# One weight conversion moved into the seam between two attention batches, and half of a scaling given to GpSimd

## The chip, the cores and the metric

The kernel runs on one core of one Trainium2 chip. The metric is the device time of one execution in microseconds; before the change it is 471.23 us (median of 3 runs, 470.49 to 472.06).

## The reference

Three blocks follow each other.

1. Attention over q, k, v of shape (2 batches, 8 heads, 576 positions, 64 wide): scores `q k^T / 8` plus a linear bias per head, masked to a causal window of 128 positions; softmax over the keys; times v.
2. A gated layer on the 1152 tokens: `a = x w1`, `b = x w2`, then `(a * b) w3 w_out`. The weights of this block arrive in float64.
3. A mixture of 8 experts: each token goes to the expert with the largest gate logit, `relu(x w1_e) w2_e`, scaled by the gate's probability.

```python
scores = np.where(mask, scale * q @ k.T + bias, -1e9)
attn = np.exp(scores - scores.max(-1)); attn /= attn.sum(-1) + 1e-9
x = attn @ v                                  # block 1
x = ((x @ w1) * (x @ w2)) @ w3 @ w_out        # block 2
out[i] = gate_w[i] * (relu(x[i] @ e1[e]) @ e2[e])   # block 3, e = argmax of the logits
```

## The kernel before

**Precision.** Matrix products of blocks 2 and 3 use a high part and a low part of each float32 operand: three products (high times high, high times low, low times high) accumulate in one PSUM bank.

**A weight conversion.** A float64 weight chunk (128 x 512) is loaded by the sync queue and turned into its two parts by `convert` (line 126). It has three pieces. `begin` (line 135) is one ScalarE instruction. `bits` (lines 138 to 140) is three VectorE instructions: a shift, an and-or, a shift-or. `parts` is a ScalarE cast that writes the high part (line 71, tile `wh`), a GpSimd subtraction that writes the low part (line 72, tile `wl`), and the issue of the next load (`stage_next`, line 101). The weights w1 and w2 make 16 chunks, four for each quarter `c` of the hidden width: two for w1 and two for w2. Four are converted during batch 0, the other twelve during batch 1. For those, the list `CONVS` (line 24) says how many each of batch 1's twelve steps takes.

**Attention steps.** Steps are numbered k = 0 to 23; batch 1 is k = 12 to 23. A step handles two heads and the row blocks (0, 1), (2, 3) or (4). Its work is spread over neighbouring steps. TensorE makes the scores one step ahead (`att_qk(k + 1)`), VectorE takes the maximum (`att_max`, line 248), ScalarE the exponential with its row sum (`att_exp`, line 259). One step later `att_norm(k)` forms the reciprocals (lines 277, 278) and, in batch 1 only, scales the probabilities: one VectorE instruction for each block and head (line 287), so four in a step with two blocks and two in a step with one. `att_tr(k)` (line 301) then transposes the probabilities on TensorE, ScalarE copies them out of PSUM (line 303) and `att_pv(k)` (line 321) multiplies by v.

**Filling work.** In batch 1 TensorE also computes block 2's first products for batch 0 (`ab_half`, lines 376 to 378), 32 units of 12 products each. Units alternate between w1 (m = 0, the result is copied by ScalarE, line 383) and w2 (m = 1, the result is multiplied into `g` by VectorE, line 388). Unit number u needs the chunks of quarter u // 8. So the first unit of quarter 1 (unit 8) falls in step 15 and unit 9, which needs quarter 1's third and fourth chunk, is the first unit of step 16; unit 16 opens step 19.

**Order.** [...] From step 14 on TensorE's order in a step is: one unit, the transposes of k - 1, the scores of k + 1, one unit (two where k % 3 is 2), the products with v of k - 1. VectorE's is: maxima of block one, scaling of k - 1, maxima of block two, then `bits`, with the g products between. GpSimd has only the subtractions of `parts` in this stretch. Step 13 is alike; the seam, k = 12, ends batch 0 (its last scaling, transposes, products with v and split of the attention output) while it begins batch 1.

Names used below: "the subtraction" is GpSimd's line 72, "the scaling" is line 287, tr(k) is the group of transposes of step k on line 301, pv(k) the products with v on line 321.

Of the kernel before, what the change touches and what calls it, by code (L numbers as in the profile page):

```python
# [20 lines left out]
BIGS = 31  # L21
STAGES = 4
WARM = (4, 4, 4, 2, 2, 2, 2, 2, 2, 2, 2)
CONVS = (0, 1, 1, 2, 1, 1, 2, 1, 1, 1, 1, 0)
OOB = 1 << 20


# [1 line left out]
def block_kernel(ctx: ExitStack, tc: tile.TileContext, qT, kT, v, w1, w2, w3T, wo, wg, e1, e2, out):  # L29
    nc = tc.nc  # L30
# [36 lines left out]
    def ps(tag, name):  # L67
        return psum.tile([P, 512], F32, tag=tag, name=name, bufs=2)
# [8 lines left out]
    def keep_clock(n, name):  # L77

        w = ps("t", name)
        for _ in range(n):  # L80
            nc.tensor.matmul(w, hot[:, :P], hot, start=True, stop=True)  # L81
# [78 lines left out]
    def load_qk(b, hp):  # L160
        h0 = 2 * hp
        t = slot(f"qk_{b}_{hp}", (2, S), F32)
        for i, src in enumerate((qT, kT)):
            nc.sync.dma_start(out=t[:, i, :], in_=src[b, h0 : h0 + 2].rearrange("h d s -> (h d) s"))
        vt = apool.tile([P, 6, P], F32, tag="v", name=f"v_{b}_{hp}", bufs=3)
        cs = slice(h0 * D, (h0 + 2) * D)
        nc.sync.dma_start(out=vt[:, 0:4, :], in_=v[b, 0 : 4 * P, cs].rearrange("(c p) d -> p c d", p=P))
        nc.sync.dma_start(out=vt[:TK, 4:6, :], in_=v[b, S - 2 * TK : S, cs].rearrange("(c p) d -> p c d", p=TK))
        qk[b, hp] = t, vt
# [38 lines left out]
    def conv_w(c, m, kp):  # L208
        if kp == 0:
            wsb[m, c] = slot(f"wh{m}_{c}", (KD, WC)), slot(f"wl{m}_{c}", (KD, WC))  # L210
        return convert(("w", c, m, kp), *(w[:, 2 * kp : 2 * kp + 2, :].rearrange("p k f -> p (k f)") for w in wsb[m, c]), pool_hi=(c == 0))
# [12 lines left out]
    def att_qk(k):  # L224
        b, hp, g = groups[k]
        t = qk[b, hp][0]
        tag = "acc" if k <= NGB and k % 2 else "s"
        sps = [ps(tag, f"s{j}_{k}").rearrange("p (i w) -> p i w", i=2) for j in range(2)]
        for gj, i in enumerate(g):
            q0, M, k0, W, _, _ = blocks[i]  # L230
            for j in range(2):
                js = slice(j * D, (j + 1) * D)
                nc.tensor.matmul(sps[j][:M, gj, :W], t[js, 0, q0 : q0 + M], t[js, 1, k0 : k0 + W], start=True, stop=True)  # L233
        live["s", k] = sps

    def att_max(k, gj):
        b, hp, g = groups[k]
        if gj == 0:
            live["p", k] = [], apool.tile([P, 12], F32, tag="sm", name=f"stat_{k}", bufs=8)
        pp, st = live["p", k]  # L240
        i = g[gj]
        q0, M, k0, W, _, _ = blocks[i]
        off = P - (q0 - k0)
        p = apool.tile([P, 2, 2 * P], F32, tag="p", name=f"p_{k}_{i}", bufs=6)
        pp.append(p)
        for j in range(2):
            c = 2 * gj + j
            nc.vector.tensor_tensor_reduce(out=p[:M, j, :W], in0=live["s", k][j][:M, gj, :W],  # L248
                                           in1=relb[:M, 2 * hp + j, off : off + W], scale=-1.0 / isq, scalar=3.0e38,
                                           op0=ALU.add, op1=ALU.min, accum_out=st[:M, c : c + 1])  # L250

    def att_exp(k, gj):
        b, hp, g = groups[k]
        pp, st = live["p", k]
        p = pp[gj]
        _, M, _, W, _, _ = blocks[g[gj]]
        for j in range(2):
            c = 2 * gj + j
            nc.scalar.activation(out=p[:M, j, :W], in_=p[:M, j, :W], func=AF.Exp, scale=-1.0,  # L259
                                 bias=st[:M, c : c + 1], accum_out=st[:M, 4 + c : 5 + c])  # L260
# [11 lines left out]
    def att_norm(k):  # L272
        b, hp, g = groups[k]
        pp, st = live["p", k]
        n = 2 * len(g)
        M = blocks[g[0]][1]
        nc.vector.tensor_scalar_add(st[:M, 8 : 8 + n], st[:M, 4 : 4 + n], 1e-9)
        nc.vector.reciprocal(st[:M, 8 : 8 + n], st[:M, 8 : 8 + n])
        if b == 0:
            for gj, i in enumerate(g):  # L280
                factor[hp, i] = st[:, 8 + 2 * gj : 10 + 2 * gj]
            return
        for gj, i in enumerate(g):
            p, W = pp[gj], blocks[i][3]
            for j in range(2):
                c = 8 + 2 * gj + j
                nc.vector.tensor_scalar_mul(p[:M, j, :W], p[:M, j, :W], st[:M, c : c + 1])

    def att_tr(k):
        b, hp, g = groups[k]  # L290
        pp, _ = live.pop(("p", k))
        pts = []
        for gj, i in enumerate(g):
            _, M, _, W, C, _ = blocks[i]
            nh = W // C
            tp = ps("t", f"t_{k}_{i}")
            pt = apool.tile([P, 2, 2, P], F32, tag="pt", name=f"pt_{k}_{i}", bufs=4)
            tpv = tp.rearrange("p (j n q) -> p j n q", j=2, n=2)
            for j in range(2):
                for n in range(nh):  # L300
                    nc.tensor.transpose(tpv[:C, j, n, :M], pp[gj][:M, j, n * C : (n + 1) * C], ident[:M, :M])  # L301
            copy = nc.vector.tensor_copy if b == 0 and i in (1, 3) else nc.scalar.copy
            copy(out=pt[:C, :, :nh, :M], in_=tpv[:C, :, :nh, :M])
            pts.append(pt)
        live["pt", k] = pts
# [52 lines left out]
    def att_fin():  # L358
        if fins:
            fins.pop(0)()  # L360
# [5 lines left out]
    def ab_half(b, f, ch, m, tag="acc", part=None):  # L366
        c, fs = f // (WC // P), slice(f * P % WC, f * P % WC + P)
        n = slice(ch * NCH, (ch + 1) * NCH)
        if part != 1:
            live["ab", m] = ps(tag, f"ab{m}_{b}_{f}_{ch}")  # L370
        a = live["ab", m]
        for kt in (range(KD), range(KD - 1), range(KD - 1, KD))[0 if part is None else 1 + part]:
            hi, lo = (w[:, kt, :] for w in wsb[m, c])
            xh, xl = xs_[b, kt]
            first, last = kt == 0, kt == KD - 1
            nc.tensor.matmul(a[:, :NCH], hi[:, fs], xh[:, n], start=first, stop=False)  # L376
            nc.tensor.matmul(a[:, :NCH], hi[:, fs], xl[:, n], start=False, stop=False)  # L377
            nc.tensor.matmul(a[:, :NCH], lo[:, fs], xh[:, n], start=False, stop=last)  # L378
        if part == 0:
            return  # L380
        if m == 0:
            asb = cv.tile([P, NCH], F32, tag="asb", name=f"asb_{b}_{f}_{ch}")
            nc.scalar.copy(out=asb, in_=a[:, :NCH])  # L383
            live["asb"] = asb
        else:
            if f % 2 == 0 and ch == 0:
                gt[b, f // 2] = slot(f"g_{b}_{f // 2}", (2, S), F32)
            nc.vector.tensor_tensor(out=gt[b, f // 2][:, f % 2, n], in0=a[:, :NCH], in1=live["asb"], op=ALU.mult)  # L388
# [259 lines left out]
    def conv_next():  # L648
        return conv_w(*wq.pop(0)) if wq else None
# [10 lines left out]
    for k in range(NGB):  # L660
# [3 lines left out]
        cvt = conv_next() if k in (2, 5, 8, 10) else None  # L664
# [36 lines left out]
    for k in range(NGB, 2 * NGB):  # L701
        b, hp, g = groups[k]
        if g[0] == 2 and hp + 2 < NPAIR:
            load_qk(1, hp + 2)
        if k == NGB:

            att_fin()
            att_norm(k - 1)
            att_tr(k - 1)
            att_pv(k - 2)  # L710
            att_pv(k - 1)

            for u in ab0[:2]:
                ab_half(*u, part=0)
            begun = ab0[:2]
            att_max(k, 0)
            att_exp(k, 0)
            att_fin()
            att_max(k, 1)
            att_exp(k, 1)  # L720
            att_fin()
            att_qk(k + 1)
            keep_clock(3, "warm_b")
            fill(ab0, 1)
        elif k == NGB + 1:
            att_soft(k, lambda: (att_norm(k - 1), fill(ab0, 1)))
            att_fin()
        else:
            att_soft(k, lambda: att_norm(k - 1))
            att_fin()  # L730
        cvts = [c for c in (conv_next() for _ in range(CONVS[k - NGB])) if c]
        for c in cvts:
            c[0]()
        if k > NGB:
            fill(ab0, 1)
            att_tr(k - 1)
        if NGB < k < 2 * NGB - 1:
            att_qk(k + 1)
        for c in cvts:
            c[1]()  # L740
        if k > NGB:
            fill(ab0, 2 if k % 3 == 2 else 1)
        for c in cvts:
            c[2]()
        if k > NGB:
            att_pv(k - 1)
# [199 lines left out]
```

## Time and profile before

| | |
|---|---|
| median of 3 runs | 471.23 us |
| the profiled execution's own time | 470.63 us |
| its span, first to last instruction | 468.9 us |
| TensorE busy | 452.7 us |
| VectorE busy | 319.9 us |
| ScalarE busy | 261.4 us |
| GpSimd busy | 147.1 us |
| mean granted TensorE clock | 0.988 |

Busy time counts an engine's instructions; an engine can be busy and yet late, where its instruction waits for a port or runs at the lower clock. The profiled execution is one of several; its own time lies 0.60 us under the median of the runs, within their spread.

### The profile page before, as it was taken

The page shows a single profiled execution, that of the slowest core. Times are in us where ns is not written, and L with a number is a line of the kernel's source. Part 1 is how long each engine was busy: PE and PEld are TensorE (multiplying, and loading weights), DVE is VectorE, ACT ScalarE, POOL GpSimd, SP SyncE. Part 2 cuts the span into 40 slices and gives each one's busy share as a digit, 9 for nine tenths or more (in the row PEclk, how much of TensorE's full clock was granted, in tenths as well). Part 3 has the DMA queues.
Part 4 walks back from the last instruction along what each step waited for, and adds up shares of the span by engine and source line. Part 5 has one row for each costly group of instructions (what it writes and reads, how often), then busy time and mean ns, then how long its engine had stood idle before and what let it go on. Part 6 is the DMA issues. An engine that isn't in the chain of part 4 may idle for free.

```text
span 468.9 us, 9276 instructions
## 1 busy us (share of the span) xinstructions
PE 452.7 (97%) x3339; PEld 405.3 (86%) x3346; DVE 319.9 (68%) x860; ACT 261.4 (56%) x653; POOL 147.1 (31%) x154
## 2 busy tenths in 40 slices
PE   8999999989999999999999999999999999999993
PEld 4667887868899999999999999588889898898982
DVE  6786768787542454888756777257878787888840
ACT  5786756565432345443545554056777677676740
POOL 2135113212111133344311211123465453544531
PEclk9999998989999999999999999999999999999998
DMA  8855325322159444675422444338796977868001
GB/s 267 248 187 177 101 85 178 113 71 87 47 176 237 132 133 136 204 298 154 146 75 69 136 136 136 114 130 275 259 288 196 310 230 248 278 205 291 27 1 54
DMA packets 30769, 77.77 MB, mean 166 GB/s; under 512 B 3582, under 2 KB 9214, under 8 KB 30720
## 3 DMA queue, kind: packets, MB, share of 16 engines
q1 hardware_dynamic: 28976, 72.41, 50.0%
q0 software_dynamic: 1744, 4.73, 2.7%
q8 instruction: 28, 0.46, 0.4%
q14 instruction: 21, 0.17, 0.1%
HBM read 65.30 MB, written 12.61 MB: 166 GB/s over the span
## 4 chain that ended last, share of the span: by engine, by line
PE 78%; DVE 10%; issue 5%; ACT 3%; POOL 2%; DVEq 0%; POOLq 0%; ACTq 0%
PE h L580 10%; PE ab L376 7%; PE ab L378 7%; PE ab L377 6%; PE h L581 4%; PE x L474 4%; PE x L475 4%; PE x L476 4%; PE warm L81 4%; DVE t_w L140 3%; PE t L301 3%; PE s L233 3%; PE oa L321 3%; PE y L609 3%; PE y L612 3%
## 5 line engine op out<-in xcount | busy, mean ns | idle before, releaser
L72 DVE TENSOR_TENSOR le<-st_e,he 128x1024 fp32r<-128x1024 f32 x64 | 78.4, 1226 | 28.1 <-ACT he L71 23.8
L376 PE MATMUL ab<-x,wh 128*128 128x288 f32 x256 | 80.3, 314 | 0.8 <-ACT wh L71 0.7
L595 POOL CAST hs<-hs 128x64 fp32r<-128x64 f32 x64 | 55.3, 871 | 76.5 <-ACT hs L591 75.3
L580 PE MATMUL h<-xs,he 128*128 128x384 f32 x256 | 76.8, 358 | 2.2 <-DVE xs L72 2.2
L378 PE MATMUL ab<-x,wl 128*128 128x288 f32 x256 | 76.4, 299 | 1.2 <-POOL wl L72 1.1
L377 PE MATMUL ab<-x,wh 128*128 128x288 f32 x256 | 76.0, 297 | 0.0
L71 ACT CAST he<-st_e 128x1024 fp32r<-128x1024 f32 x64 | 67.3, 1051 | 0.0
L581 PE MATMUL h<-xs,le 128*128 128x192 f32 x256 | 64.2, 251 | 0.0
L376 PEld LDWEIGHTS ab<-x,wh 128*128 128x128 f32 x256 | 48.6, 190 | 6.4 <-issue 2.3
L580 PEld LDWEIGHTS h<-xs,he 128*128 128x128 f32 x256 | 48.0, 188 | 5.2 <-DVE xs L72 2.6
L581 PEld LDWEIGHTS h<-xs,le 128*128 128x128 f32 x256 | 48.8, 191 | 1.9
L378 PEld LDWEIGHTS ab<-x,wl 128*128 128x128 f32 x256 | 48.6, 190 | 2.0 <-POOL wl L72 2.0
L377 PEld LDWEIGHTS ab<-x,wh 128*128 128x128 f32 x256 | 48.7, 190 | 0.0
L388 DVE TENSOR_TENSOR g<-ab,asb 128x288 f32<-128x288 f32 x32 | 14.6, 456 | 48.0 <-PE ab L378 45.7
L259 ACT ACTIVATE p<-p,stat 128x256 f32<-128x256 f32 (+2 forms) x80 | 37.3, 470 | 13.0 <-DVE stat L248 13.0
L474 PE MATMUL x<-wph,gh 128*128 128x260 f32 x144 | 41.4, 287 | 0.0
L476 PE MATMUL x<-wph,gl 128*128 128x260 f32 x144 | 40.6, 282 | 0.0
L475 PE MATMUL x<-wpl,gh 128*128 128x260 f32 x144 | 40.6, 282 | 0.0
L588 ACT COPY cr<-h 128x192 f32<-128x192 f32 x64 | 20.5, 320 | 35.3 <-PE h L581 33.2
L383 ACT COPY asb<-ab 128x288 f32<-128x288 f32 x32 | 12.7, 397 | 47.8 <-PE ab L378 47.8
L440 PE MATMUL wp<-woh,w3h 128*128 128x260 f32 x128 | 36.3, 284 | 0.5 <-DVE wpl L72 0.5
L442 PE MATMUL wp<-woh,w3l 128*128 128x260 f32 x128 | 36.2, 283 | 0.0
(139 smaller groups left out, 1074.5 us busy)
## 6 DMA issues: line engine op xcount, KB each, us to landing
st_e<-e SPq DMA_DIRECT2D x64, 512.0 KB, 4.3
st_w<-w SPq DMA_DIRECT2D x16, 512.0 KB, 4.5
st_w<-w3T SPq DMA_DIRECT2D x16, 512.0 KB, 4.0
disp<-zrow SPq DMA_DIRECT2D x1, 4626.0 KB, 22.1
st_wo<-wo SPq DMA_DIRECT2D x8, 512.0 KB, 3.6
qk<-qT SPq DMA_DIRECT2D x8, 288.0 KB, 5.2
qk<-kT SPq DMA_DIRECT2D x8, 288.0 KB, 5.6
y<-zrow SPq DMA_DIRECT2D x1, 2304.0 KB, 10.9
```

The source lines that it names most:

```text
L71: nc.scalar.copy(out=hi, in_=t)
L72: eng.tensor_tensor(out=lo, in0=t, in1=hi.bitcast(F32), op=ALU.subtract)
L259: nc.scalar.activation(out=p[:M, j, :W], in_=p[:M, j, :W], func=AF.Exp, scale=-1.0, bias=st[:M, c : c + 1], accum_out=st[:M, 4 + c : 5 + c])
L376: nc.tensor.matmul(a[:, :NCH], hi[:, fs], xh[:, n], start=first, stop=False)
L377: nc.tensor.matmul(a[:, :NCH], hi[:, fs], xl[:, n], start=False, stop=False)
L378: nc.tensor.matmul(a[:, :NCH], lo[:, fs], xh[:, n], start=False, stop=last)
L474: nc.tensor.matmul(pa[:, :HG], gh[:, kt, :], th, start=(kt == 0), stop=False)
L475: nc.tensor.matmul(pa[:, :HG], gh[:, kt, :], tl, start=False, stop=False)
L476: nc.tensor.matmul(pa[:, :HG], gl[:, kt, :], th, start=False, stop=(kt == KF - 1))
L580: nc.tensor.matmul(hp_[:, : 2 * N0], hi[:, kt, fs], xs, start=(kt == 0), stop=False)
L581: nc.tensor.matmul(hp_[:, N0 : 2 * N0], lo[:, kt, fs], xs[:, :N0], start=False, stop=(kt == KD - 1))
L595: nc.gpsimd.tensor_copy(h[:, 2 * N0 :], h[:, P:N0])
```

## The change

`CONVS` changes, so that batch 1 converts two chunks in a step once (step 14) and no longer twice (steps 15 and 18). The first of the twelve is taken in the seam, with its three pieces at three places between the seam's softmax parts. And in the scaling of batch 1 the second head of each block (j = 1) is given to GpSimd, the first stays on VectorE.

```diff
-CONVS = (0, 1, 1, 2, 1, 1, 2, 1, 1, 1, 1, 0)
+CONVS = (0, 1, 2, 1, 1, 1, 1, 1, 1, 1, 1, 0)
...
                 c = 8 + 2 * gj + j
-                nc.vector.tensor_scalar_mul(p[:M, j, :W], p[:M, j, :W], st[:M, c : c + 1])
+                (nc.gpsimd if j else nc.vector).tensor_scalar_mul(p[:M, j, :W], p[:M, j, :W], st[:M, c : c + 1])
...
             begun = ab0[:2]
+            cvt = conv_next()
+            cvt[0]()
             att_max(k, 0)
             att_exp(k, 0)
+            cvt[1]()
             att_fin()
             att_max(k, 1)
             att_exp(k, 1)
             att_fin()
+            cvt[2]()
             att_qk(k + 1)
```

Chunks converted by the end of each step of batch 1, k = 12 to 22: before 0, 1, 2, 4, 5, 6, 8, 9, 10, 11, 12; after 1, 2, 4, 5, 6, 7, 8, 9, 10, 11, 12.

## Rows read from the trace of the kernel before

**Rows 1.** The page: TensorE's granted clock in 40 slices, tenths.
```profile
PEclk9999998989999999999999999999999999999998
```

**Rows 2.** Windows of 2 us: busy by engine, granted clock, DMA share, GB/s.
```profile
72.00:74.00 2.00, 1.94 (x10) 1.57 (x9) 2.00 (x7) 0.69 (x3) 0.60 (x1) 0.55 1.08 327
...
96.00:98.00 2.00, 2.00 (x9) 1.13 (x10) 1.97 (x9) 1.53 (x5) 0.00 (x0) 0.52 0.00 0
```

**Rows 3.** Timeline of TensorE: start, us, line, tile; idle before and its releaser.
```profile
65.87 0.37 PE L301 MATMUL t<-ident,p 64*96 64x64 f32 x3
...
68.92 0.46 PE L321 MATMUL ob<-pt,v 96*64 96x64 f32 x8
...
71.41 0.40 PE L378 MATMUL ab<-x,wl 128*128 128x288 f32 x1 [0.82 <-POOL wl L72]
...
73.78 1.48 PE L301 MATMUL t<-ident,p 128*128 128x128 f32 x6
...
77.63 0.93 PE L321 MATMUL oa<-pt,v 128*64 128x128 f32 x12
...
91.29 0.46 PE L321 MATMUL ob<-pt,v 96*64 96x64 f32 x8
...
95.52 1.46 PE L301 MATMUL t<-ident,p 128*128 128x128 f32 x6 [1.99 <-DVE p L287]
...
100.30 0.93 PE L321 MATMUL oa<-pt,v 128*64 128x128 f32 x12
...
113.97 0.46 PE L321 MATMUL ob<-pt,v 96*64 96x64 f32 x8
116.07 0.81 PE L301 MATMUL t<-ident,p 128*128 128x128 f32 x6
...
119.06 0.93 PE L321 MATMUL oa<-pt,v 128*64 128x128 f32 x12
```

**Rows 4.** Timeline of VectorE at three places and of ScalarE at one, the second.
```profile
45.73 0.69 DVE L351 TENSOR_TENSOR rs<-oa,rs 128x512 f32<-128x512 f32 x1 [2.71 <-ACT rs L349]
...
50.10 0.40 ACT L383 COPY asb<-ab 128x288 f32<-128x288 f32 x1 [1.52 <-PE ab L378]
...
91.20 1.62 DVE L140 SCALAR_TENSOR_TENSOR t_w<-t_w,x_w 128x512 int32<-128x512 int32 x1
...
93.79 1.04 DVE L277 TENSOR_SCALAR stat<-stat 128x4 f32<-128x4 f32 x1
```

**Rows 5.** Timeline of GpSimd: subtractions of four conversions.
```profile
64.16 1.30 POOL L72 TENSOR_TENSOR wl<-t_w,wh 128x512 fp32r<-128x512 f32 x1 [7.44 <-ACT wh L71]
...
91.00 1.27 POOL L72 TENSOR_TENSOR wl<-t_w,wh 128x512 fp32r<-128x512 f32 x1 [4.83 <-ACT wh L71]
93.55 1.26 POOL L72 TENSOR_TENSOR wl<-t_w,wh 128x512 fp32r<-128x512 f32 x1 [1.28 <-ACT wh L71]
...
115.13 1.45 POOL L72 TENSOR_TENSOR wl<-t_w,wh 128x512 fp32r<-128x512 f32 x1 [4.62 <-ACT wh L71]
```

**Rows 6.** Instructions of lines 138, 140, 287: count, duration ns min/median/max.
```profile
L138 DVE TENSOR_SCALAR x_w<-st_w x32: 407/419/1474, 13.2 to 233.1; 128x512 int32<-128x512 int32 x32
...
L140 DVE SCALAR_TENSOR_TENSOR t_w<-t_w,x_w x32: 691/693/1625, 14.5 to 234.3; 128x512 int32<-128x512 int32 x32
...
L287 DVE TENSOR_SCALAR p<-p,stat x40: 275/346/1443, 50.4 to 127.5; 128x256 f32<-128x256 f32 x24, 128x128 f32<-128x128 f32 x8, 64x192 f32<-64x192 f32 x8
```

**Rows 7.** Groups of GpSimd by form: count, busy us, mean ns.
```profile
L72 POOL TENSOR_TENSOR wl<-t_w,wh 128x512 fp32r<-128x512 f32 x12 | 15.7, 1310 | 61.9 <-ACT wh L71 61.9
...
L145 POOL CAST wh<-t_w 128x512 fp32r<-128x512 f32 x4 | 2.4, 609 | 13.7 <-DVE stat L277 11.3 <-DVE t_w L140 2.4
...
L177 POOL TENSOR_SCALAR_AFFINE_SELECT iota<-iota 128x256 f32<-128x256 f32 x1 | 0.4, 398 | 0.1
```

**Rows 8.** Windows of 1 us around two short waits of TensorE; columns as in rows 2.
```profile
305.00:306.00 1.00, 0.23 (x4) 0.09 (x2) 0.31 (x1) 0.82 (x2) 0.00 (x0) 1.00 0.97 293
...
317.00:318.00 1.00, 0.18 (x1) 0.18 (x2) 1.00 (x4) 0.00 (x0) 0.13 (x1) 1.00 0.90 369
```

## The prediction

> **What bounds the kernel now.** I read the page's busy times first. TensorE's 452.7 us of 468.9 make it the bound nearly everywhere, so what an edit is worth is what TensorE gains or loses in the stretch that the edit touches, and whatever moves TensorE there moves the end: after batch 1 it works through without a gap that another engine's earlier work could fill. The page's line of the granted clock comes next [rows 1]: slices 7 and 9 (70 to 82 and 94 to 105 us) stand at 8, inside batch 1. Windows show what this is: from 72 to 74 us the mean clock is 0.55, from 96 to 98 us 0.52 [rows 2], which is the lower of its two levels (1.2 GHz) nearly throughout.
>
> Then the timeline of TensorE. Steps come in threes, and the same work stands three times in batch 1: from pv of a one-block step to the transposes of the next two-block step (8 small products, one unit), and from there to the next pv (6 transposes, 4 scores, one unit). Undisturbed (step 21 to 22) these take 116.07 - 113.97 = 2.10 us and 119.06 - 116.07 = 2.99 us [rows 3]. Around step 16 they take 73.78 - 68.92 = 4.86 and 77.63 - 73.78 = 3.85; around step 19 they take 95.52 - 91.29 = 4.23 and 100.30 - 95.52 = 4.78 [rows 3]. Both disturbed places follow a step with two conversions. At the first, unit 9 waits for the low part that GpSimd subtracts (0.82 us at 71.41, one of three such waits). At the second, the transposes wait 1.99 us for the scaling on VectorE [rows 3], and the timeline of VectorE says why that is late: a conversion's last instruction took 1.62 us from 91.20, beside GpSimd's subtraction of 91.00 to 92.27, and the reciprocal's first one 1.04 us from 93.79, until the second subtraction was over at 94.81 [rows 4, 5].
>
> The surplus is what the two places cost: (4.86 - 2.10) + (3.85 - 2.99) = 3.62 us and (4.23 - 2.10) + (4.78 - 2.99) = 3.92 us, together 7.54 us. Of it 0.86 + 1.79 is the second stretch of each, in which nothing waits long and the clock is low.
>
> **The change part by part.**
>
> *The conversions spread anew.* Quarter 1's third and fourth chunk are now converted in step 14, a whole step before unit 9 asks for them (its wait was on subtractions that began after 70 us; the last one is now due near 67). Step 18 has one conversion, so one subtraction less stands beside VectorE's reciprocals, and VectorE loses three instructions there (0.42 + 0.69 + 0.69 = 1.80 us by the medians of lines 138 and 140, the middle one priced like the last [rows 6]). Both waits go, and with them the low clock: -7.54 us. What is late next is the scaling that GpSimd now does, below.
>
> *The seam's conversion.* Its 1.80 us of `bits` stand on VectorE between 43.0 and 45.73, where it waited 2.71 us for ScalarE's copies [rows 4]. That leaves 0.91 us for a delay of the shift by a subtraction of the attention output that GpSimd has at the start of that time; more would be seen. The cast falls into ScalarE's wait of 1.52 us before 50.10 [rows 4]. The subtraction (1.28 us) then runs into VectorE's next reciprocals and delays scaling and transposes by 0 to 0.3 us. The load it issues comes a step earlier, into a buffer long free; nothing on the sync queue waits behind it. I take 0; without the cover the price is the 1.80 us.
>
> *Two conversions in step 14.* The three extra VectorE instructions must be done before ScalarE's cast, and that stands behind its copy of unit 6 anyway: the subtraction began at 64.16 [rows 5]. There is no cost there, but the second subtraction lengthens GpSimd's queue by 1.28 us, to 66.75.
>
> *The second head's scaling on GpSimd.* 20 VectorE instructions go (median 0.346, best 0.275 us each [rows 6]); VectorE is not the bound once the double steps are gone, so this is worth 0 on TensorE. What counts is when GpSimd has done its 20. The trace of before has no such instruction. Its nearest rows: a cast of 128x512 at 0.609 and a one-input select of 128x256 at 0.398 us below, half the two-input subtraction of 128x512, 0.655 us, above [rows 7]. It has one tensor input, so I take 0.40 us for 256 columns and 0.30 for 128.
>
> In GpSimd's order this scaling of step k stands behind the subtraction of step k, which waits for ScalarE's cast, which waits for the copy of the unit before. So, step by step:
> - tr(14): the second subtraction ends at 66.75, the scaling at about 67.10; the transposes began at 65.87 [rows 3], and half of them (head one) don't wait: about 1.0 us.
> - tr(15) and tr(21): the subtraction of step 21 began at 115.13, 1.16 us after pv began at 113.97 [rows 3, 5]. With 1.28 us it ends at 2.44 on that scale, the two scalings at 2.75 and 3.15; the transposes start at 2.10 and their last two are due at about 2.5. The wait is 0.65 us each, 1.3 in all.
> - tr(12), (13), (16), (18), (19), (22): the subtraction is done earlier. Four scalings by turns on the two engines take about 2 x 0.28 + 2 x 0.40 = 1.36 us, where four on VectorE took 1.14; the surplus of 0.2 and small waits for the queue come to 0.8 us over the six. tr(17), (20), (23): 0.
>
> That is 1.0 + 1.3 + 0.8 = 3.1 us of new waiting, none over 1.2 us. Waits of TensorE of that size left the clock where it was: beside waits of 0.77 us in window 305 and 0.82 in window 317 it stands at 1.00 [rows 8], while the fall to about half followed the larger ones of rows 3. I take no loss of clock.
>
> By turns is itself read from the trace: lines 138, 140 and 287 have a median of 0.42, 0.69 and 0.35 us, and a maximum of 1.47, 1.63 and 1.44 [rows 6]; two such stretched instructions lie beside a subtraction [rows 4, 5]. The Trainium skill (SBUF — State Buffer, Who interferes with whom) says that VectorE and GpSimd share a pair of ports under an exclusive lock, held for a whole instruction, and that tensor_scalar in a two-port mode and an operation with two SBUF inputs take part in it. The trace agrees: 1.62 us for an instruction whose median is 0.69. By this rule splitting the scaling over two engines does not halve it; without it the four would take about 0.80 us and the six small waits would fall away, 0.8 us less in the sum.
>
> **Sum.** 470.63 - 7.54 + 3.1 = 466.2 us against the profiled execution. That lies 0.60 us under the median of the runs; half of this added for the runs to come gives 466.5 us.
>
> **The rivals.**
> 1. *GpSimd's scaling takes more, or its waits bring the clock down again* (a smaller gain). At 0.655 us, 13 scalings that TensorE sees (one in step 14, two each in steps 15 and 21, two each in four of the others) cost 13 x 0.25 = 3.3 us more: 469.5. Or tr(14) and tr(15), 1.0 and 0.65 us some 5 us apart, lower the clock once, for 0.86 to 1.79 us: 467 to 468; twice, with tr(21): 470. For it: the queue order is certain. Against it: the one-input rows and rows 8.
> 2. *Slower: GpSimd becomes the bound of batch 1.* The same 13 scalings at a price p add 3.1 + 13 (p - 0.40) us. This eats the whole gain from p = 0.74 and makes the kernel slower by over 1.4 us from about p = 0.85. At 1.27, the price of the two-input subtraction of 512 columns, it adds 14.4: 477.5 before any loss of clock, which would fall at each of the three steps. For it: a scaling by a value for each row is not in the trace. Against it: every row with one tensor input is near 1 ns a column.
> 3. *The low clock and both waits go and nothing new is seen.* If the transposes' first half and ScalarE's copies absorb the new waits: 470.63 - 7.54 = 463.1 (463.4 by the runs). Against it: tr(14) has 1.28 us of queue in front of it that no row hides.
> 4. *It doesn't do what it says*: the two-conversion step only takes its stall along, from steps 15 and 18 to step 14, 3.6 us once, with the new waits on top: 470.63 - 7.54 + 3.62 + 3.1 = 469.8. Against it: in step 14 VectorE has only one block of maxima, TensorE one unit more, and no unit wants the chunks before step 16.
>
> The Trainium skill (GPSIMD Engine Reference, Engine selection) holds one-input work on GpSimd to be near line rate and two-input work about twice as slow as on VectorE. Rows 7 agree (609 against 1310 ns for 512 columns). By its first half p is near 0.40.
>
> **How the numbers follow.** The forecast (464.5 to 468.5) has 0.56, rival 1 has 0.20, rival 2 has 0.09, rival 3 has 0.08, rival 4 has 0.07. A measurement of this kernel can tell about 0.3% (1.4 us) from no change: faster is under 469.8, slower over 472.6. All of the forecast and of rival 3, two thirds of rival 1 and half of rival 4 are faster: 0.56 + 0.08 + 0.13 + 0.03 = 0.80; I lower it to 0.76 since the price p is in no row. Slower is 0.09. The rest, 0.15, is the same. The range, 463.1 to 470.5, takes in rival 3's end and rival 1's and leaves out rival 2 and the edges, some 0.15 to 0.2.
>
> **What would show it.** Right: the granted clock is 1.00 in all windows from 66 to 105 us; the first stretch after pv(14) and after pv(17) falls from 4.86 and 4.23 to 2.1 to 2.9 us and the second to about 3.0; a wait of TensorE on line 301 for GpSimd's line 287 of about 1 us stands at step 15 (near 66 us), of 0.6 at steps 16 and 22; GpSimd's line 287 has a mean under 0.5 us; from about 130 us every mark is 4 to 5 us earlier. Wrong: GpSimd's mean over 0.7 us; clock under 0.9 in a window of this stretch; a wait of TensorE in the seam (43 to 52 us) on VectorE's split of the attention output, which would mean that the seam's conversion had no cover.

## The result, and the profile after

The changed kernel takes 478.01 us (median of 6 runs, 477.63 to 479.28) against 471.30 us before: ratio 1.0144, 95% interval 1.0130 to 1.0158. It is 6.7 us slower; 466.5 was forecast, 4.7 us faster.

The instructions of line 287, by engine (count, duration min/median/max in ns); GpSimd's mean by shape is in the second fence (busy us, mean ns).

```profile
L287 DVE TENSOR_SCALAR p<-p,stat x20: 285/348/570, 51.4 to 133.9; 128x256 f32<-128x256 f32 x12, 128x128 f32<-128x128 f32 x4, 64x192 f32<-64x192 f32 x4
L287 POOL TENSOR_SCALAR p<-p,stat x20: 654/920/1393, 51.6 to 134.1; 128x256 f32<-128x256 f32 x12, 128x128 f32<-128x128 f32 x4, 64x192 f32<-64x192 f32 x4
```

```profile
L287 POOL TENSOR_SCALAR p<-p,stat 128x256 f32<-128x256 f32 x12 | 13.1, 1102 | 1.2 <-DVE p L287 0.8 <-DVE stat L278 0.4
```

A scaling takes GpSimd 0.92 us in the median over its shapes and 1.10 us in the mean for 256 columns, where VectorE takes 0.35 in the median; the prediction took 0.40. TensorE's waits, from 40 to 150 us, say what follows:

```profile
PE t L301 <- POOL p L287: 8.4, 13, 1.5
PE ab L378 <- POOL wl L72: 0.3, 1, 0.3
```

13 waits of the transposes for GpSimd, 8.4 us, took the place of those of before (1.99 us of the transposes, 0.67 and 0.82 of unit 9). TensorE's timeline, with the lines that answer to [rows 3] (all marks are 0.64 us late from the first scores on, at 5.89 instead of 5.25 us, since the twelve products of line 81 ahead of them take 4.70 us instead of 4.06; intervals don't contain this):

```profile
65.03 1.15 PE L321 MATMUL oa<-pt,v 128*64 128x128 f32 x16
...
67.90 0.31 PE L301 MATMUL t<-ident,p 64*96 64x64 f32 x2
69.69 0.26 PE L301 MATMUL t<-ident,p 64*96 64x64 f32 x1 [1.48 <-POOL p L287]
...
72.63 0.46 PE L321 MATMUL ob<-pt,v 96*64 96x64 f32 x8
74.70 0.27 PE L301 MATMUL t<-ident,p 128*128 128x128 f32 x1
75.95 0.55 PE L301 MATMUL t<-ident,p 128*128 128x128 f32 x3 [0.97 <-POOL p L287]
77.32 0.44 PE L301 MATMUL t<-ident,p 128*128 128x128 f32 x2 [0.83 <-POOL p L287]
...
79.96 0.93 PE L321 MATMUL oa<-pt,v 128*64 128x128 f32 x12
...
116.30 0.46 PE L321 MATMUL ob<-pt,v 96*64 96x64 f32 x8
118.40 0.27 PE L301 MATMUL t<-ident,p 128*128 128x128 f32 x1
119.62 0.55 PE L301 MATMUL t<-ident,p 128*128 128x128 f32 x3 [0.95 <-POOL p L287]
120.99 0.47 PE L301 MATMUL t<-ident,p 128*128 128x128 f32 x2 [0.83 <-POOL p L287]
...
125.12 0.93 PE L321 MATMUL oa<-pt,v 128*64 128x128 f32 x12
```

Two things are to be seen. The first stretch, pv of a one-block step to the next transposes, is healed: 74.70 - 72.63 = 2.07 us, from 4.86. And the transposes themselves now stop twice in a step, once for each of GpSimd's two scalings: the second stretch grew from 3.85 to 79.96 - 74.70 = 5.26 us at step 16, and at step 22, which was the undisturbed 2.99 before, to 125.12 - 118.40 = 6.72. There the clock fell too (window of 2 us; busy by engine, clock, DMA share, GB/s):

```profile
122.00:124.00 2.00, 2.00 (x9) 1.77 (x8) 1.49 (x8) 0.14 (x1) 0.00 (x0) 0.50 0.64 246
```

GpSimd's timeline shows the queue: the subtraction, then both scalings without a gap.

```profile
117.46 1.30 POOL L72 TENSOR_TENSOR wl<-t_w,wh 128x512 fp32r<-128x512 f32 x1 [4.17 <-ACT wh L71]
118.74 2.20 POOL L287 TENSOR_SCALAR p<-p,stat 128x128 f32<-128x128 f32 x2
```

They end at 120.94, and the last transposes start at 120.99.

### The profile page after: what moved, and what is told of

It reads as the page before. It is cut to its first block, busy times and chain, and to the rows that moved or that the text cites. A ratio compares the mean times of both kernels' runs of the same rounds, so it can differ in the third digit from the quotient of the medians.

```text
span 476.4 us, 9305 instructions
## 1 busy us (share of the span) xinstructions
PE 455.1 (96%) x3346; PEld 404.2 (85%) x3346; DVE 314.7 (66%) x840; ACT 261.9 (55%) x653; POOL 165.5 (35%) x174
## 3 DMA queue, kind: packets, MB, share of 16 engines
q1 hardware_dynamic: 28976, 72.41, 49.5%
## 4 chain that ended last, share of the span: by engine, by line
PE 71%; DVE 11%; issue 7%; POOL 5%; ACT 4%; POOLq 0%; DVEq 0%; ACTq 0%
PE h L580 10%; PE ab L376 6%; PE ab L378 5%; PE ab L377 5%; PE h L581 4%; PE warm L81 4%; PE x L474 4%; PE x L475 4%; PE x L476 4%; POOL p L287 3%; DVE t_w L140 3%; PE y L609 3%; PE y L612 3%; PE y L610 3%; PE y L613 3%
```

## The experiments

Theory A: the loss is all GpSimd's scaling, by its price and its place in GpSimd's queue; the new spread and the seam do what they say. Theory B: the spread takes its stall along and the seam has no cover.

**1. The new spread and the seam alone** (e1_spread_only)

```diff
-                (nc.gpsimd if j else nc.vector).tensor_scalar_mul(...)
+                nc.vector.tensor_scalar_mul(...)
```

> The changed kernel with the whole scaling back on VectorE; seam conversion and new spread stay. Theory A (the loss is all GpSimd's scaling, at about 0.9 us for 256 columns instead of the 0.40 that the prediction took; seam and spread do what they say): both waits and the low clock go, 471.3 - 7.5 = 463.8 us, 463 to 465. Theory B (the spread only moves its stall, as two conversions in step 14 crowd ScalarE and VectorE, and the seam delays the start of batch 1): 469 us or more.

Measured: 466.38 us, ratio 0.9885 (0.9849 to 0.9921), 4.5 us faster than before and 11.6 faster than the changed kernel. B is out; A holds in its sign, though the gain is 3 us short of 7.5. The scores of step 13 follow the first scores of the kernel by 48.59 - 6.06 = 42.53 us, as before (47.78 - 5.25): the seam cost TensorE nothing. The timelines of TensorE and, below, of VectorE with one line of GpSimd show where the rest is:

```profile
64.00 1.14 PE L321 MATMUL oa<-pt,v 128*64 128x128 f32 x16
...
69.92 0.46 PE L321 MATMUL ob<-pt,v 96*64 96x64 f32 x8
...
72.00 1.05 PE L301 MATMUL t<-ident,p 128*128 128x128 f32 x6
72.98 0.85 PE L233 MATMUL s<-qk 64*64 64x192 f32 x4
...
75.57 0.93 PE L321 MATMUL oa<-pt,v 128*64 128x128 f32 x12
...
78.52 0.63 PE L301 MATMUL t<-ident,p 128*128 128x128 f32 x4 [0.23 <-DVE p L287]
...
91.82 1.09 PE L301 MATMUL t<-ident,p 128*128 128x128 f32 x6
...
95.38 0.93 PE L321 MATMUL oa<-pt,v 128*64 128x128 f32 x12
...
109.69 0.46 PE L321 MATMUL ob<-pt,v 96*64 96x64 f32 x8
...
114.78 0.93 PE L321 MATMUL oa<-pt,v 128*64 128x128 f32 x12
```

```profile
70.51 2.05 DVE L287 TENSOR_SCALAR p<-p,stat 128x128 f32<-128x128 f32 x4
71.08 1.33 POOL L72 TENSOR_TENSOR wl<-t_w,wh 128x512 fp32r<-128x512 f32 x1 [3.38 <-ACT wh L71]
72.48 0.41 DVE L248 CUSTOM_DVE_ANT_0 p<-s,relb 128x256 f32<-128x256 f32 x1
...
89.91 0.46 DVE L388 TENSOR_TENSOR g<-ab,asb 128x288 f32<-128x288 f32 x1 [1.44 <-PE ab L378]
...
91.38 1.01 DVE L287 TENSOR_SCALAR p<-p,stat 128x128 f32<-128x128 f32 x4
...
96.50 1.21 DVE L277 TENSOR_SCALAR stat<-stat 128x4 f32<-128x4 f32 x1
```

The first stretch is 2.08 us, near the undisturbed 2.10 of [rows 3], but the second is 75.57 - 72.00 = 3.57 us instead of 2.99 (95.38 - 91.82 = 3.56 at step 19), and from pv(15) to tr(16) and pv(18) to tr(19) it is 2.95 and 3.08, where 2.57 and 2.56 stood before. VectorE's four scalings of step 16 took 2.05 us, where they take 1.01 without one beside them: a subtraction of GpSimd ran from 71.08 to 72.41. The maxima come after them, and the next scores (0.85 us instead of 0.54) need the bank that the maxima read. Step 19 is another case: its scalings took 1.01 us, and its stretch is long all the same. There VectorE waited 1.44 us for a unit's result, to be multiplied into `g` at 89.91, before it could begin the maxima. In front of tr(19) it was the reciprocal's first instruction (line 277) that took 1.21 us, beside a subtraction from 96.40 to 97.69; it takes 0.16 without one.

**2. GpSimd's scaling alone, conversions as before** (e2_gpsimd_only)

```diff
-                nc.vector.tensor_scalar_mul(...)
+                (nc.gpsimd if j else nc.vector).tensor_scalar_mul(...)
```

> The kernel before with only the second head's scaling on GpSimd; conversions as before. Theory A: the loss stands by itself. In the changed kernel it was 478.0 - 463.8 = 14.2 us; here some of the waits fall on those that are there anyway (steps 16 and 19), so 480 to 486 us. Theory B: about 471 us, or 2 us more at most, as only the small waits of taking turns are added.

Measured: 479.76 us, ratio 1.0157 (1.0117 to 1.0197): 8.8 us slower, a little under A's range and far from B. The two parts don't add up: -4.5 + 8.8 = 4.3, the whole change gives 6.7 to 7.1. Step 14's second subtraction is part of this: tr(14) waits 1.48 us behind it in the changed kernel and not at all here.

**3. Without the seam's conversion** (e3_no_seam)

```diff
-CONVS = (0, 1, 1, 2, 1, 1, 2, 1, 1, 1, 1, 0)
+CONVS = (0, 2, 2, 1, 1, 1, 1, 1, 1, 1, 1, 0)
```

This is the only edit against the kernel before: nothing is converted in the seam, and the whole scaling is on VectorE.

> As the run with the new spread alone, but the seam's conversion is taken in step 13 (two conversions in steps 13 and 14). Theory A in its full form (every doubled step before a two-block step makes the low part or the scaling late): tr(13) in step 14 waits for the scaling behind two conversions, as tr(18) did before, and the time is 2 to 4 us above the run with the seam, 466 to 468 us. Rival (the seam is not needed; only the chunks' due date and step 18 counted): within 0.7 us of it.

Measured: 467.89 us, ratio 0.9906 (0.9868 to 0.9943). The intervals of this run and of run 1 overlap; the trace decides: the transposes of step 13 wait for VectorE's scaling, and from pv(12) at 56.85 it is 3.80 us, against 2.62 in run 1.

```profile
60.65 1.15 PE L301 MATMUL t<-ident,p 128*128 128x128 f32 x8 [1.10 <-DVE p L287]
```

So a doubled step in front of a two-block one costs 1.2 us there, in kind as A had it and less than its 2 to 4 us, and the seam saves that.

**4. The subtraction behind the scaling, scaling on GpSimd** (e4_sub_behind; lines are numbered one higher)

```diff
+LATE = (14, 15, 16, 20, 21)
...
+        for c in late:
+            c[2]()
+        late = []
...
+        if k in LATE:
+            late = cvts
+        else:
+            for c in cvts:
+                c[2]()
```

> The changed kernel, but after steps 14, 15, 16, 20 and 21 the third piece of a conversion (cast, subtraction, next load) is put behind the next step's scaling, so that GpSimd's scaling no longer queues behind the subtraction there. If the queue order is the larger half of the loss: tr(14), tr(15), tr(16), tr(20), tr(21) lose their waits of about 1.5, 1.8, 0.9, 0.5 and 1.8 us, and the time falls by 5 to 7 us plus the low clock after step 22, to 470 to 473. If the price itself is the larger half: under 3 us, 475 or more.

Measured: 472.12 us, ratio 1.0012 (0.9996 to 1.0029): 5.9 us under the changed kernel. Queue order is half of the 11.6 us that line 287 costs.

```profile
PE t L302 <- POOL p L288: 3.4, 9, 0.7
...
PE ab L379 <- POOL wl L73: 0.8, 1, 0.8
```

The transposes' waits for GpSimd fall from 8.4 to 3.4 us, none over 0.7, and the granted clock is 1.00 in all windows of 4 us from 40 to 144 us. ScalarE's cast was moved together with the subtraction; no run separates the two.

**5. The price by itself** (e5_price): GpSimd works on an unused tile at the start of the kernel before, where nothing waits for it.

```diff
...
+    for n in (128, 192, 256):
+        nc.gpsimd.tensor_scalar_mul(pa[:, :n], pa[:, :n], desc[:, :1])
+    for n in (128, 256):
+        nc.gpsimd.tensor_scalar_mul(pa[:, :n], pa[:, :n], 0.5)
+    for n in (128, 256):
+        nc.gpsimd.tensor_copy(pa[:, :n].bitcast(F32R), pa[:, :n])
+    nc.gpsimd.tensor_tensor(out=pa[:, :128], in0=pa[:, :128], in1=pa[:, 128:], op=ALU.mult)
```

> The kernel before with extra work on GpSimd at about 4 us, where it is idle: the scaling by a value for each row on 128, 192 and 256 columns, by a constant on 128 and 256, a cast on 128 and 256, a two-input product on 128; none of it is used. If the price of the scaling is its own: about 0.66, 0.78 and 0.91 us as the shortest in the changed kernel, against 0.29 and 0.40 for the cast, whatever runs beside it. If it is mostly waiting for the port: near the cast's. The constant's price tells whether the value for each row is what costs (then 0.3 to 0.4) or the operation (then as the first three).

Measured (one execution, 470.68 us; busy us, mean ns):

```profile
L206 POOL TENSOR_SCALAR probe<-probe,desc 128x256 f32<-128x256 f32 x1 | 0.9, 922 | 0.1
L208 POOL TENSOR_SCALAR probe<-probe 128x256 f32<-128x256 f32 x1 | 0.8, 848 | 0.1
L206 POOL TENSOR_SCALAR probe<-probe,desc 128x192 f32<-128x192 f32 x1 | 0.8, 763 | 0.1
L206 POOL TENSOR_SCALAR probe<-probe,desc 128x128 f32<-128x128 f32 x1 | 0.7, 718 | 0.1
L208 POOL TENSOR_SCALAR probe<-probe 128x128 f32<-128x128 f32 x1 | 0.5, 528 | 0.1
L211 POOL TENSOR_TENSOR probe<-probe 128x128 f32<-128x128 f32 x1 | 0.5, 458 | 0.1
L210 POOL CAST probe<-probe 128x256 fp32r<-128x256 f32 x1 | 0.4, 400 | 0.1
...
L210 POOL CAST probe<-probe 128x128 fp32r<-128x128 f32 x1 | 0.3, 289 | 0.1
```

The price is the operation's own: 0.92 us with 256 columns, and 0.85 with a constant, where a cast has 0.40. The three scalings by a value for each row run from 4.25 to 6.85 us, and VectorE is idle until 7.44. With 128 columns it is dearer than a product of two tensors.

**6. The subtraction behind the scaling, scaling on VectorE** (e6_late_vector): run 4's order, after steps 13 to 16 and 19 to 21, with run 1's line 287.

> The new spread alone (scaling on VectorE), with the third piece of a conversion put behind the next step's scaling after steps 13 to 16 and 19 to 21. If the 3 us that the new spread alone stayed short of 7.5 are VectorE's scaling held by GpSimd's subtraction (it took 2.05, 2.09 and 2.24 us at three places, against 1.01 to 1.14): 464 us, 463.5 to 465. Rival (TensorE's scores wait for VectorE's maxima anyway, whichever instruction holds these up): 466 to 467.

Measured: 467.68 us, ratio 0.9927 (0.9903 to 0.9951); the expected 464 failed. At one place the mechanism shows: pv(18) to tr(19) is 97.99 - 95.43 = 2.56 us, from 3.08 in run 1. But the pieces that were put off now come late themselves, with these waits for a low and a high part:

```profile
PE ab L379 <- POOL wl L73: 0.8, 1, 0.8
PE ab L377 <- ACT wh L72: 0.4, 1, 0.4
```

And the rival holds where the stretch was to be mended. VectorE's scalings take 1.01 us at steps 16 and 19, and from the transposes to the next pv it is still 75.49 - 71.93 = 3.56 us at both:

```profile
71.49 1.01 DVE L288 TENSOR_SCALAR p<-p,stat 128x128 f32<-128x128 f32 x4
...
71.93 1.08 PE L302 MATMUL t<-ident,p 128*128 128x128 f32 x6 [0.63 <-DVE p L288]
```

At step 16 two put-off subtractions, from 66.41 to 69.13, now run beside VectorE's `bits`, one instruction of which takes 1.67 us instead of 0.69.

Compared with run 4, the scaling on GpSimd costs 472.12 - 467.68 = 4.4 us in this order, where it costs 478.01 - 466.38 = 11.6 with the subtraction in front. (The late steps of the two differ by 13 and 19.)

**7. The second head's scaling on ScalarE** (e7_scalar)

```diff
+                if j:
+                    nc.scalar.activation(out=p[:M, j, :W], in_=p[:M, j, :W], func=AF.Copy, scale=st[:M, c : c + 1])
+                else:
+                    nc.vector.tensor_scalar_mul(...)
```

> The new spread, the second head's scaling on ScalarE in place of GpSimd. A copy with a scale on ScalarE should take about 0.5 us for 256 columns and shares no port, so VectorE has two scalings fewer in front of the next maxima: 464 to 466 us. Rival: ScalarE is full around the exponentials of two-block steps (100% in two windows of 2 us), so its scalings come late and the transposes wait: 467 us or more.

Measured: 466.64 us, ratio 0.9899 (0.9877 to 0.9920), not told apart from run 1 and between the two outcomes expected. The scores are at 0.54 us again, but the transposes wait for ScalarE instead (lines are numbered three higher there):

```profile
PE t L304 <- ACT p L288: 1.3, 2, 0.7
```

**8. Both** (e8_late_scalar): runs 6 and 7 together.

> Both: the second head's scaling on ScalarE and the third piece of a conversion behind the next scaling. If port and order are what is left: 463 to 464.5 us, the least of all. Rival as in the run before: ScalarE's queue is the bound, 466 us or more.

Measured: 466.72 us, ratio 0.9903 (0.9879 to 0.9928). Expected was 463 to 464.5; it failed. The two waits that the trace shows, of unit 25 for its low part as in run 6 and of tr(15) for VectorE's scaling, are 1.4 of the 2.2 us or more that are missing:

```profile
PE ab L382 <- POOL wl L73: 0.8, 1, 0.8
PE t L305 <- DVE p L291: 0.6, 1, 0.6
```

**9. Step 22's conversion moved to step 17** (e9_two_in_17), otherwise run 1

```diff
-CONVS = (0, 1, 2, 1, 1, 1, 1, 1, 1, 1, 1, 0)
+CONVS = (0, 1, 2, 1, 1, 2, 1, 1, 1, 1, 0, 0)
```

> The new spread with the scaling on VectorE, and the conversion of step 22 moved to step 17 (two there, none in 22), so that unit 25 and tr(22) no longer stand behind a subtraction. Undisturbed, pv(21) to tr(22) took 2.57 us elsewhere and 3.13 there. If that is what it costs and step 17, with one block and two units, hides a second conversion as step 14 does: 0.5 us less than 466.4, so 465.9. Rival: the second subtraction in step 17 holds tr(18), so that it is even or up to 1 us slower, 466.4 to 467.4.

Measured: 467.03 us, ratio 0.9901 (0.9886 to 0.9917): the rival's outcome; no gain. Both sides show in the trace: pv(21) to tr(22) is 118.63 - 116.09 = 2.54 us, from 3.13, and pv(16) to pv(17) is 91.04 - 84.61 = 6.43, from 5.92. The loss stands in front of pv(17), not of tr(18).

**10. Runs 8 and 9 with fewer late steps** (e10_scalar_17): late after steps 15, 16 and 18 to 21.

> As the run before, with the second head's scaling on ScalarE and the third piece of a conversion behind the next scaling after steps 15, 16 and 18 to 21 (no longer 13 and 14, after which unit 9 waited 0.8 us for its low part). From the marks of the run with both, 466.7: 0.75 us back at step 16, 0.5 at step 23, so 465.4 us. Rival: ScalarE's exponentials stand before the cast in the late piece, and the low part of unit 17 or 25 comes late again: 466 to 467.

Measured: 465.95 us, ratio 0.9884 (0.9865 to 0.9902). It is not told apart from run 1 (0.9849 to 0.9921). The wait of 0.8 us that this expectation puts down to unit 9 was unit 25's (116.97 us in run 8); behind steps 13 and 14 it was tr(15) that waited. The best version found is the change without its line 287, 466.4 us.

## Why the prediction was wrong

**The step that failed** is the price of GpSimd's scaling: "It has one tensor input, so I take 0.40 us for 256 columns and 0.30 for 128." Measured alone it is 0.92 and 0.72 (run 5), in the kernel 1.10 in the mean. The bracket "half the two-input subtraction of 128x512, 0.655 us, above" was no upper bound either: it was reasoned from the number of inputs, and no row showed this operation. Nor do [rows 7] put "every row with one tensor input" near 1 ns a column: the cast has 609 / 512 = 1.2 and the select 398 / 256 = 1.6. What makes the mean in the kernel 0.18 us longer than the price alone was not separated. The sentence beside rows 7, from the Trainium skill (GPSIMD Engine Reference, Engine selection), that one-input work is near line rate, holds here for the cast (0.40 us for 256 columns) and not for the scaling. [Rows 7] compare GpSimd with itself; its 1310 ns for two inputs stand against 0.69 us of VectorE in [rows 4].

**The mechanism was rival 2's**, put at 0.09. Its formula, 3.1 + 13 (p - 0.40) us, gives 9.9 us at p = 0.92, and with the gain as forecast 470.63 - 7.54 + 9.9 = 473.0 us, slower. The loss of clock that it expected at three steps came at one. Between the changed kernel and run 1, which differ in line 287 alone, TensorE's marks, each counted from the kernel's first scores, show what it was (after: 5.89, run 1: 6.06 us):

| up to | lag of the changed kernel, us | added by | forecast, us |
|---|---|---|---|
| pv(13) | (65.03 - 5.89) - (64.00 - 6.06) = 1.2 | tr(13): 1.2 | some of 0.8 |
| pv(14) | (72.63 - 5.89) - (69.92 - 6.06) = 2.9 | tr(14): 1.7 | 1.0 |
| pv(15) | (79.96 - 5.89) - (75.57 - 6.06) = 4.6 | tr(15): 1.7 | 0.65 |
| pv(20) | (116.30 - 5.89) - (109.69 - 6.06) = 6.8 | tr(16) to tr(20): 2.2 | the rest of 0.8 |
| pv(21) | (125.12 - 5.89) - (114.78 - 6.06) = 10.5 | tr(21) and the clock: 3.7 | 0.65 |

The last two steps of batch 1 add about 0.6; the whole is 11.1 us of the 11.6 measured. The places were forecast, all but tr(20) (0.3 us); each was dearer, from 1.7 times at tr(14) to nearly six at tr(21). Run 1 is itself a little long at some of them: against the undisturbed 2.99 us, tr(15) costs 5.26 - 2.99 = 2.3.

**"I take no loss of clock"** was wrong at one place: after tr(21) it stood at 0.50. The single waits there, 0.95 and 0.83 us, are about as short as those of [rows 8], where it held; but there are two of them within 2.3 us, with three transposes between. [Rows 3] had spoken against the step: the wait at 71.41, 0.82 us (with one of 0.67 ahead of it), is no larger than those of [rows 8], and the clock fell behind it [rows 2]. The same pair at step 16 (0.97 and 0.83) left it at 1.00. What tells these two apart is open: TensorE was busy for 1.05 and 1.17 us in the windows of 2 us from 118 and 120 us, and for 1.03 and 1.17 us in those from 74 and 76.

**The gain of 7.54 us** was too large by about 2.45. From the first scores to pv(23) the kernel before takes 131.34 - 5.25 = 126.09 us and run 1 127.06 - 6.06 = 121.00, 5.09 less. The waits went, as said: both first stretches are at 2.1 us in the changed kernel and in runs 1, 3, 7, 9 and 10 (in 4, 6 and 8, which put subtractions off, step 16's is 2.5 to 2.9). But "What is late next is the scaling that GpSimd now does" missed that VectorE is next even where it keeps the scaling. In run 1 the subtraction holds its scalings at tr(15) (2.05 us instead of 1.01) and tr(16) (2.09 instead of 1.14), and the reciprocal's first instruction at tr(13) (0.77 instead of 0.36) and tr(19) (1.21 instead of 0.16). From pv to pv these places are 0.6, 0.5, 0.2 and 0.6 us longer than forecast, together 1.9.

The other 0.57 us is step 19's second stretch, 3.56 us in runs 1, 3, 6 and 9 alike. There "the same work stands three times" does not hold for VectorE. Units alternate and three steps take seven, so step 19's first maxima stand right behind a product into `g`, those of steps 16 and 22 behind `bits`. So 2.99 us was no measure of step 19, and 0.57 us of the surplus of 1.79 there was no stall; this is read from the traces, and no run moved the units. Step 22 was also no test of the hold: its subtraction began at 115.13, near the end of the scalings, and was itself the longer one (1.45 us [rows 5]). Runs 6 to 10 tried to win the rest back by order, engine and spread, and moved the wait each time.

**What was right.** The seam's conversion cost TensorE nothing up to pv(12) (run 1) and spared 1.2 us at tr(13) (run 3). Two conversions in step 14 disturbed no unit. That the two engines take turns fits the changed kernel: VectorE's two scalings of tr(13) took 0.84 us from 57.69, beside GpSimd's from 57.83, and the two of tr(16) 0.62 us from 79.23, with GpSimd idle.

## What to carry to other kernels

An instruction that no row of the trace shows on its new engine has no price until it has run there: the number of its inputs did not bound it, and one execution of it in an idle place (run 5) would have turned this forecast round (473.0 us by rival 2's formula). Before work is moved to an engine with a free share, read what stands ahead of it in that engine's queue at each place; the same instructions cost 11.6 us behind the subtractions and 4.4 us where those of five steps were put behind them (the two runs compared for this differ by the late steps 13 and 19). And when a stall is removed, follow the producer's chain past it for the next wait before its whole surplus is booked as gain, and see that the place taken as undisturbed has the same work on every engine that feeds the bound.

## What the runs showed of the hardware

GpSimd's scaling takes 0.72, 0.76 and 0.92 us on 128, 192 and 256 columns of float32 with a value for each row, 0.53 and 0.85 us on 128 and 256 with a constant, and its cast 0.29 and 0.40 us (run 5): from 128 to 256 columns a scaling by a constant grows by 2.5 ns a column, a cast by 0.9. VectorE does the same scaling of up to 256 columns in 0.35 us in the median.

VectorE's scalings are stretched by a GpSimd subtraction that runs beside them, to 2.05 us for four that take 1.01 without it (run 1). The lock that the Trainium skill describes (SBUF — State Buffer, Who interferes with whom) fits; VectorE's custom maxima, which read PSUM and one SBUF tensor, are not stretched, as that page has it for an instruction with one SBUF input: in run 1 two of them take 0.34 us each from 56.63, beside a subtraction that begins there too, and 0.34 each from 76.11 with GpSimd idle.
